# Two layers of one-token attention over a cache: uneven last rows of four loads, and W2's end laid over its start so that more keys stay

## The chip, the cores and the metric

The kernel runs on one core of one Trainium2 chip. Times are microseconds on the device. "Before" is the median of three runs, 1355.34 (1352.47 to 1356.29). A profile is one further execution, recorded by the hardware profiler.

## The reference

One token passes through two equal layers that share all weights and the cache. Each layer is attention with 32 heads over 8192 cached positions, then a small MLP:

```python
q = (layernorm(x) @ wq)                        # 640 -> 32 heads x 128
p = softmax(q . k_cache * 128 ** -0.5)         # per head, 8192 positions
x = x + (p @ v_cache) @ wo                     # 4096 -> 640
x = x + relu(layernorm(x) @ w1) @ w2           # 640 -> 1728 -> 640
```

All is float32. K and V of one head are 4 MiB each, so each layer reads 256 MiB of cache. Layer 1 walks the heads backwards, from 31 to 0, so that what layer 0 read last can stay in the chip's memory and serve layer 1 first.

## The kernel before

**The ring.** K, V and most of W2 are loaded into one big tile, `ring`, by SP's DMA queue (line 204). Its space is counted in *places* of 8 floats in each of 128 partitions, 4 KB. A head's data are cut into *units*, and a unit into *pieces*: a K piece `(r, c, n)` holds positions c to c+n of run r (four runs of 512 columns, for four groups of positions); a V piece holds a block of rows. Heads 2 to 26 are one unit of eight pieces of 256 places each, loaded in stretches of up to 64 KB per partition (`turning`); the other heads have several units. The table `UNITS` (lines 42 to 61) writes them out by hand, and the same table sets the layout in HBM, so that each load reads whole rows of up to 64 KB.

**What sets the order.** `todo` lists the loads in order. `pump` (line 190) issues from its head as long as the ring has room: at a fixed place (`turning`) or where `place` (line 166) finds a gap. Each `scores` and `values` call that has used a piece calls `release`, which frees its places and pumps again. So a load on SP's queue waits for PE's last use of the places that it overwrites, and for landed loads that the tile framework makes it wait for; everything behind it on SP's queue waits too. WQ and WO for groups of four heads come by ACT's queue.

**Kept heads.** `KEPT = 3800` places (lines 62, 63) hold heads 31 and most of 30 from layer 0 to layer 1. The rest of head 30's K, two units of 216 and 80 places' worth of columns, is loaded a second time at the boundary of the layers, into the tiles `mix` and `wct`, which are then free (`load_beside`, lines 806 and 845). `RING = KEPT + 960`: the last 960 places hold the twelve blocks of W2 that pass through the ring (80 places each, four runs of 4, 4, 2 and 2 blocks).

**The boundary.** When head 31's V has been used, the MLP follows: `hidden` with the last head's output (L603), WO of the last head and W2 by `times_rows` (L419), the ReLU (L824 to L850). W2's blocks are used in the order 0 to 3, two that have a tile of their own, 4 to 11 (line 859). Each use frees 80 places, into which layer 1's first loads (head 29) go. Then come the layer norm and the queries of layer 1, and the scores of head 31 from kept keys (L448).

**Compute.** Per head PE multiplies q with K (L448), DVE and ACT do the softmax (L459 to L489), PE multiplies with V (L497), DVE gathers (L512, L516). Other PE work is put between the heads.

Of the kernel before, what the change touches and what calls it, by code (L numbers as in the profile page):

```python
# [16 lines left out]
D = 640  # L17
H = 32
SK = 8192
DH = 128  # L20
DFF = 1728
# [24 lines left out]
UNITS[29] = [  # L46
    ("k", K_ALL[:1]),
    ("k", K_ALL[1:2]),
    ("k", [(2, 0, 512), (3, 0, 384)]),
    ("v", V_ALL[:1]),  # L50
    ("v", V_ALL[1:2]),
    ("k", [(3, 384, 128)]),
    ("v", V_ALL[2:3]),
    ("v", V_ALL[3:]),
]
UNITS[30] = [
    ("k", [(0, 432, 80), (1, 0, 80)]),
# [1 line left out]
    ("k", [(1, 80, 432)] + K_ALL[2:]),  # L59
] + HALVES[2:]  # L60
UNITS[31] = HALVES[:2] + LAST
DROPPED = {30: 2}
KEPT = 3800
MIX_AT = [12, 16, 20, 24]
AHEAD = 3

# [5 lines left out]
def kind_of(unit, t):  # L72

    return unit[0] if unit[0] != "kv" else "k" if t < len(K_ALL) else "v"


def wide(kind, piece):

    if kind == "w":
        return D // 8  # L80
    return 4 * piece[2] * (1 if kind == "k" else DH) // 8


def size(unit):
    return sum(wide(kind_of(unit, t), piece) for t, piece in enumerate(unit[1]))
# [4 lines left out]
F_TILES = 3  # L90
# [2 lines left out]
W2_RUNS = [range(0, 4), range(4, 8), range(8, 10), range(10, 12)]  # L93
UNITS["w2"] = [("w", list(run)) for run in W2_RUNS]
W2_ALL = [("w2", i) for i in range(len(W2_RUNS))]
RING = KEPT + 4 * F_TILES * D // 8


@with_exitstack
def decode_kernel(ctx: ExitStack, tc: tile.TileContext, x, kv, wq, wo, w1, w2, w2_rest, out):  # L100
    nc = tc.nc
# [11 lines left out]

    ring = consts.tile([P, 8 * RING], F32, name="ring")
    order = [(h, i) for h in range(H) for i in range(len(UNITS[h]))]
    kept = [u for u in order if u[0] >= min(DROPPED) and u[1] >= DROPPED.get(u[0], 0)]
    assert sum(size(UNITS[h][i]) for h, i in kept) == KEPT
    beside = [(1, u) for u in order if u[0] == 30 and u not in kept]
    todo = []

    def all_of(layer, u):
# [34 lines left out]
    source = {}  # L156
    for us, dram in ((order, kv), (W2_ALL, w2)):
        o = 0
        for u in us:
            n = 8 * P * size(UNITS[u[0]][u[1]])  # L160
# [5 lines left out]
    def place(layer, u, n):  # L166

        step = 512 if n % 512 == 0 else 8
        if layer:
            low, high = 0, RING  # L170
        elif u[0] in range(FULL[0]):
            low, high = 0, 16 * SLOT
        elif u[0] == "w2":
            low, high = KEPT, RING
        else:
            low, high = (3072, KEPT) if n == KEPT - 3072 else (0, 3072)
        at, best = low, None
        for a, m in sorted(live.values()) + [(high, 0)]:
            a = min(a, high)
            for base in (0, KEPT):  # L180
                c = base + -(-max(at - base, 0) // step) * step
                if a - c >= n and (best is None or a - at < best[1]):
                    best = c, a - at
            at = max(at, a + m)
        return None if best is None else best[0]

    def is_free(at, n):
        return all(a >= at + n or a + m <= at for a, m in live.values())

    def pump():  # L190
        while todo:
            layer, u, first, last, at = todo[0]
            unit = UNITS[u[0]][u[1]]
            ns = [wide(kind_of(unit, t), piece) for t, piece in enumerate(unit[1])]
            n = sum(ns[first:last])
            if at is None:
                at = place(layer, u, n)
                if at is None:
                    return
            elif not is_free(at, n):  # L200
                return
            todo.pop(0)
            o = 8 * sum(ns[:first])
            nc.sync.dma_start(ring[:, 8 * at : 8 * (at + n)], source[u][:, o : o + 8 * n])
            for t in range(first, last):
                live[layer, u, t] = at, ns[t]
                at_of[layer, u, t] = ring, 8 * at
                at += ns[t]

    def load_beside(where, at, n):  # L210
        layer, u = beside.pop()
        kind, pieces = UNITS[u[0]][u[1]]
        assert 8 * size(UNITS[u[0]][u[1]]) == n
        nc.sync.dma_start(where[:, at : at + n], source[u])
        for t, piece in enumerate(pieces):
            at_of[layer, u, t] = where, at
            at += 8 * wide(kind, piece)

    def key(L, u, t):
        return (0 if u in kept else L), u, t  # L220

    def release(L, u, t):
        if (L or u not in kept) and at_of[key(L, u, t)][0] is ring:
            del live[key(L, u, t)]
            pump()
# [13 lines left out]
    def load_wq(g, queue):  # L239
        wq_t[g] = wts.tile([P, NB, HG * DH], F32, name="wq_t")  # L240
        queue.dma_start(wq_t[g], wq[g])
# [3 lines left out]
        queue.dma_start(wo_t[g], wo[g])  # L245

    xr = work.tile([P, DR], F32, name="xr", bufs=2)
    nc.sync.dma_start(xr, x)
    load_wq(0, nc.sync)
    pump()  # L250
    load_wo(0, nc.sync)

# [23 lines left out]
    mix = consts.tile([P, DFF], F32, name="mix")  # L276
# [54 lines left out]
    def deviations(xt, s):  # L331
        pt = ps_m.tile([P, 512], F32, name="pm")
        nc.tensor.matmul(pt[:, :1], all_rows, s, start=True, stop=True)
        m = work.tile([P, 1], F32, name="ln_m")
        nc.vector.tensor_scalar(m, pt[:, :1], 1.0 / D, 0.0, op0=ALU.mult, op1=ALU.add)
        xc = work.tile([P, 2 * DH], F32, name="q_row")[:, :DR]
        nc.vector.tensor_scalar(xc, xt, m, 0.0, op0=ALU.subtract, op1=ALU.add)
        ss = work.tile([P, 1], F32, name="ln_ss")
        nc.vector.scalar_tensor_tensor(
            xc, xc, 1.0, xc, op0=ALU.mult, op1=ALU.mult, accum_out=ss  # L340
        )
        return ss

    def spread_of_rows(ss):
        pv = ps_m.tile([P, 512], F32, name="pm")
        nc.tensor.matmul(pv[:, :1], all_rows, ss, start=True, stop=True)
        return inv_std(pv[:, :1])
# [68 lines left out]
    def times_rows(acc, wt, col, first, last):  # L416

        for g in range(4):
            nc.tensor.matmul(  # L419
                acc[32 * g : 32 * g + 32, :DR],  # L420
                col.to_broadcast([col.shape[0], 32]),
                wt[:, g * DR : (g + 1) * DR],
                start=first,
                stop=last,
                skip_group_check=True,
            )
# [103 lines left out]
    def copied_rows(hd):  # L530

        rows = work.tile([P, 4, DH], F32, name="p")
        nc.vector.tensor_copy(rows[:, :2], hd.out[:, :2])
        nc.scalar.copy(rows[:, 2:], hd.out[:, 2:])
        return rows
# [64 lines left out]
    def hidden(ph, col, wt, first, last):  # L600
        for g in range(4):
            f, n = F_AT[g], F_ROWS[g]
            nc.tensor.matmul(  # L603
                ph[32 * g : 32 * g + 32, :n],
                col.to_broadcast([P, 32]),
                wt[:, f : f + n],
                start=first,
                stop=last,
                skip_group_check=True,
            )  # L610

    def attention_and_mlp(L, xr, s):
        heads = list(range(H))[:: 1 - 2 * L]
        last = heads[-1]
        runs = [heads[a : a + HG] for a in range(0, H, HG)]
        groups = [run[0] // HG for run in runs]
# [106 lines left out]
        for where, h in enumerate(heads[:-1]):  # L723
# [36 lines left out]
            k, j = divmod(where, HG)  # L760
# [36 lines left out]
        rows = copied_rows(hd)  # L797
        keep_busy(1, 128)
        o = work.tile([P, 1], F32, name="c_ol")
# [2 lines left out]

        xp, ph = mlp_in
        hidden(ph, o, mix, False, True)
        if L == 0:
            load_beside(mix, 0, DFF)
        pd = ps_m.tile([P, 512], F32, name="pm")
        times_rows(pd, wo_t[last // HG][:, last % HG], o, True, True)
        keep_busy(1, 128)
# [50 lines left out]
        for a, b in enumerate(blocks):  # L860
            if a == 2:
                ss = deviations(x1, s1)
            if a == 8:
                r1 = spread_of_rows(ss)
            rows = 2 * half if b == nb + 1 else P
            if b < nb:
                i = next(i for i, run in enumerate(W2_RUNS) if b in run)
                where = L, ("w2", i), b - W2_RUNS[i][0]
                tile_of, at = at_of[where]
                wt = tile_of[:, at : at + D]  # L870
            else:
                wt = w2_t[:rows, b - nb]
            times_rows(po, wt, hT[:rows, b : b + 1], a == 0, a == len(blocks) - 1)
            if b < nb:
                release(*where)

        x2 = work.tile([P, DR], F32, name="xr", bufs=2)
        s2 = work.tile([P, 1], F32, name="x_s", bufs=2)
# [7 lines left out]
    for L in range(2):  # L886
        xr, s = attention_and_mlp(L, xr, s)
# [80 lines left out]
```

## Time and profile before

| | |
|---|---|
| median of three runs | 1355.34 us |
| the profiled execution's own time | 1351.49 us |
| its span, first to last instruction | 1349.7 us |
| granted clock of TensorE | 0.81 |
| PE, DVE, ACT busy | 59%, 19%, 4% of the span |
| SP's DMA queue (q1) | 20312 packets, 531.89 MB |
| ACT's DMA queue (q10) | 4608 packets, 42.44 MB |

How to read it. The profile has a share of time in which the core's 16 DMA engines moved packets, for the span in 40 slices or for any stretch: 1.00 means that all 16 are busy, 0.50 that half of them are, or all of them half the time. The chain of waits is followed back from the last instruction to what released it. "us to landing" is the time from a DMA's issue to its last byte; most of it is standing in the queue behind older loads. The queues named "instruction" carry the program's own code.

### The profile page before, as it was taken

The numbers are of one execution on the slowest core, as the hardware profiler recorded it, in microseconds if no ns is written. First come the engines' busy times: TensorE is split into PE (matmuls) and PEld (weight loads), VectorE is DVE, ScalarE is ACT, GpSimd is POOL, SyncE is SP. The second block draws the span as 40 slices with busy tenths as digits, with TensorE's granted clock in tenths as the row PEclk, the third lists the DMA queues.
The fourth block names the chain that finished last, engine by engine and source line by source line (L and its number), as shares of the span: only waits on it lengthen the run. The fifth ranks groups of instructions, "written<-read, shape, count | busy, mean of one in ns | idle before, by whom it ended". The sixth has DMA issues, their size and how long they took to land.

```text
span 1349.7 us, 13544 instructions
## 1 busy us (share of the span) xinstructions
PE 799.3 (59%) x6048; PEld 270.4 (20%) x6048; DVE 251.4 (19%) x794; ACT 59.2 (4%) x149; POOL 2.9 (0%) x10
## 2 busy tenths in 40 slices
PE   5455555554654655457787754555566554656658
PEld 2011111211211211122242211111121121212214
DVE  1111111221211211122122211122111211111212
ACT  0000000000000000000000000000000000000000
POOL 0000000000000000000000000000000000000000
PEclk8777677878978976788799777797778778777879
DMA  9999999999999999999999999999999999999997
GB/s 392 445 419 437 432 428 441 417 431 436 439 426 432 430 435 422 448 417 420 425 405 423 435 431 432 432 431 436 438 434 424 421 435 443 429 420 438 429 418 322
DMA packets 24977, 575.17 MB, mean 426 GB/s; under 512 B 2772, under 2 KB 2904, under 8 KB 5336
## 3 DMA queue, kind: packets, MB, share of 16 engines
q1 hardware_dynamic: 20312, 531.89, 91.8%
q10 hardware_dynamic: 4608, 42.44, 7.5%
q8 instruction: 47, 0.77, 0.2%
q14 instruction: 10, 0.08, 0.0%
HBM read 574.31 MB, written 0.00 MB: 426 GB/s over the span
## 4 chain that ended last, share of the span: by engine, by line
DMA 65%; PE 27%; DVE 5%; issue 1%; ACT 1%; ACTq 0%; SPq 0%; DVEq 0%
DMA ring<-in_kv 64%; PE ps L448 13%; PE outs L497 8%; DVE h_t L459 2%; PE px L387 1%; DVE pt L477 1%; PE pm L464 1%; ACT p L473 1%; DMA wo_t<-in_wo 1%; DVE p L516 1%; PE acc L419 1%; PE px L419 1%; PE acc L603 0%; PE px L590 0%; DVE pT L479 0%
## 5 line engine op out<-in xcount | busy, mean ns | idle before, releaser
L448 PE MATMUL ps<-ring,spread_q 128*32 128x512 f32 (+2 forms) x2072 | 331.0, 787 | 334.5 <-DMA ring<-in_kv 329.6
L497 PE MATMUL outs<-ring,pT 128*4 128x512 f32 (+1 forms) x2080 | 268.2, 658 | 27.7 <-DVE pT L479 17.4
L448 PEld LDWEIGHTS ps<-ring,spread_q 128*32 128x32 f32 x2072 | 76.9, 138 | 523.2 <-issue 298.4
L459 DVE TENSOR_REDUCE h_t<-ps 128x1 f32<-128x512 f32 x64 | 44.3, 692 | 640.3 <-PE ps L448 640.3
L473 ACT ACTIVATE p<-ps,h_t 128x512 f32<-128x512 f32 x64 | 44.0, 687 | 1226.4 <-DVE h_t L471 1226.4
L497 PEld LDWEIGHTS outs<-ring,pT 128*4 128x4 f32 x2080 | 52.5, 92 | 184.4 <-issue 156.9
L526 PE MATMUL pm<-ones,p 128*128 128x1 f32 x120 | 22.9, 260 | 94.8 <-DVE p L516 94.8
L512 DVE TENSOR_SCALAR p<-outs,ind 128x128 f32<-128x128 f32 x60 | 21.1, 351 | 248.2 <-PE outs L497 248.2
L516 DVE SCALAR_TENSOR_TENSOR p<-outs,ind,p 128x128 f32<-128x128 f32 x180 | 63.1, 351 | 6.4
L477 DVE STREAM_TRANSPOSE pt<-p 128x512 f32<-128x512 f32 x64 | 46.5, 727 | 57.9 <-ACT p L473 57.9
L464 PE MATMUL pm<-row_of,h_t 128*128 128x16 f32 x128 | 25.7, 276 | 49.9 <-DVE h_t L459 49.0
L526 PEld LDWEIGHTS pm<-ones,p 128*128 128x128 f32 x120 | 17.8, 188 | 151.5 <-DVE p L516 149.9
L464 PEld LDWEIGHTS pm<-row_of,h_t 128*128 128x128 f32 x128 | 19.4, 190 | 109.2 <-DVE h_t L459 107.3
L590 PE MATMUL px<-w_t,wct 128*128 128x448 f32 (+1 forms) x80 | 36.6, 573 | 1.1 <-ACT wct L583 1.1
L387 PE MATMUL px<-wq_t,ln_xc 128*32 128x256 f32 x280 | 32.9, 381 | 0.0
L486 PE MATMUL pm<-ind,h_t 128*128 128x1 f32 x128 | 23.4, 252 | 15.3 <-ACT p L473 15.3
L486 PEld LDWEIGHTS pm<-ind,h_t 128*128 128x128 f32 x128 | 23.2, 207 | 34.1 <-ACT p L473 26.6
L419 PE MATMUL acc<-wo_t,o_cols 128*32 128x160 f32 x496 | 22.7, 324 | 0.6 <-DVE o_cols L544 0.6
L527 DVE TENSOR_SCALAR o_cols<-pm,h_t 128x1 f32<-128x1 f32 x60 | 13.1, 218 | 30.6 <-PE pm L526 30.6
L387 PEld LDWEIGHTS px<-wq_t,ln_xc 128*32 128x32 f32 x280 | 15.2, 109 | 12.7 <-issue 1.2
L471 DVE TENSOR_REDUCE h_t<-pm 128x1 f32<-128x16 f32 x64 | 11.2, 175 | 32.4 <-PE pm L464 32.4
L419 PEld LDWEIGHTS acc<-wo_t,o_cols 128*32 128x32 f32 x496 | 15.8, 117 | 4.8 <-issue 2.5
(110 smaller groups left out, 201.2 us busy)
## 6 DMA issues: line engine op xcount, KB each, us to landing
ring<-in_kv SPq DMA_DIRECT2D x20, 4096.0 KB, 34.5
ring<-in_kv SPq DMA_DIRECT2D x38, 2048.0 KB, 29.3
ring<-in_kv SPq DMA_DIRECT2D x11, 6144.0 KB, 38.2
wq_t<-in_wq ACTq DMA_DIRECT2D x14, 1280.0 KB, 23.4
wo_t<-in_wo ACTq DMA_DIRECT2D x14, 1280.0 KB, 23.8
ring<-in_kv SPq DMA_DIRECT2D x15, 1024.0 KB, 16.7
ring<-in_w SPq DMA_DIRECT2D x4, 1280.0 KB, 26.8
w_t<-in_w ACTq DMA_DIRECT2D x1, 4320.0 KB, 47.7
```

The source lines that it names most:

```text
L387: nc.tensor.matmul(pq[32 * j : 32 * j + 32, :n], xc[:, c : c + 1].to_broadcast([P, 32]), wq_t[g][:, c, j * n : (j + 1) * n], start=(c == 0 ...
L419: nc.tensor.matmul(acc[32 * g : 32 * g + 32, :DR], col.to_broadcast([col.shape[0], 32]), wt[:, g * DR : (g + 1) * DR], start=first, stop=last,
L448: nc.tensor.matmul(hd.ps[32 * g : 32 * g + 32, c : c + n], spread_q[:, 3 - r : 35 - r], tile_of[:, at + g * n : at + (g + 1) * n], start=f ...
L459: nc.vector.tensor_reduce(hd.nm, hd.ps, AX.X, ALU.max, negate=True)
L464: nc.tensor.matmul(pt[:, :16], hd.nm.to_broadcast([P, P]), row_of.rearrange("p g r -> p (g r)"), start=True, stop=True,)
L473: nc.scalar.activation(hd.p, hd.ps, AF.Exp, bias=hd.low, scale=1.0, accum_out=hd.l)
L477: nc.vector.transpose(pt, hd.p)
L486: nc.tensor.matmul(pt[:, :1], hd.l.to_broadcast([P, P]), ind[:, 4:5], start=True, stop=True)
L497: nc.tensor.matmul(hd.out[32 * g : 32 * g + 4, r : r + m].rearrange("p r d -> p (r d)"), hd.pT[:, 4 * i : 4 * i + 4], tile_of[:, v : v + m ...
L516: nc.vector.scalar_tensor_tensor(oc[:, r], hd.out[:, r], ind[:, r : r + 1], oc[:, r - 1], op0=ALU.mult, op1=ALU.add,)
L526: nc.tensor.matmul(pt[:, :1], oc[:, 3], ones, start=True, stop=True)
L590: nc.tensor.matmul(pt[:, :n], wct[:, c], w1_t[:, c, f : f + n], start=(c == 0), stop=(c == NB - 1),)
```

## The change

Five edits.

1. *More kept.* Head 29's K is cut anew, so that its last 320 columns of run 3 are a unit of their own, `(29, 9)`, of 160 places, loaded last. It is kept: `DROPPED` gains `29: 9`, `KEPT` goes from 3800 to 3960. Layer 1 doesn't load it again. The older K unit of 448 places becomes two of 128 and 160.
2. *W2 over itself.* `RING` is `KEPT + 800`: the same 4760 places in all. W2's last run (blocks 10 and 11) has no room until blocks 0 and 1 are used, in layer 0; then it goes over them.
3. *The second loads of head 30.* `beside` is turned round: wct's load comes first, at the place where it was; mix's, which was issued after `hidden`, comes after W2's second block.
4. *Uneven division.* Four loads (heads 9 and 15, in both layers) are split: all but the last 256 or 128 places of the stretch go in one DMA of 128 rows; those last places go in three DMAs of 64, 63 and 1 rows, or of 64, 51 and 13.
5. *x* is loaded by ACT's queue and not by SP's.

`place` and `apart` give the new units fixed homes. The core of the diff:

```diff
-    ("k", [(2, 0, 512), (3, 0, 384)]),
+    ("k", [(2, 0, 256)]),
+    ("k", [(2, 256, 256), (3, 128, 64)]),
...
-    ("k", [(3, 384, 128)]),
+    ("k", [(3, 0, 128)]),
...
+    ("k", [(3, 192, 320)]),
...
-DROPPED = {30: 2}
-KEPT = 3800
+DROPPED = {29: 9, 30: 2}
+KEPT = 3960
+W2_PLACES = 800
+SHARED = {
+    (0, 9): (SK // 32, [64, 63, 1]),
+    (0, 15): (SK // 64, [64, 51, 13]),
+    (1, 15): (SK // 32, [64, 63, 1]),
+    (1, 9): (SK // 64, [64, 51, 13]),
+}
...
-RING = KEPT + 4 * F_TILES * D // 8
+RING = KEPT + W2_PLACES
...
-            nc.sync.dma_start(ring[:, 8 * at : 8 * (at + n)], source[u][:, o : o + 8 * n])
+            tail, groups = SHARED.get((layer, u[0]), (0, [])) if last == len(unit[1]) else (0, [])
+            nc.sync.dma_start(
+                ring[:, 8 * at : 8 * (at + n - tail)], source[u][:, o : o + 8 * (n - tail)]
+            )
+            p = 0
+            for rows in groups:
+                nc.sync.dma_start(
+                    ring[p : p + rows, 8 * (at + n - tail) : 8 * (at + n)],
+                    source[u][p : p + rows, o + 8 * (n - tail) : o + 8 * n],
+                )
+                p += rows
...
-    nc.sync.dma_start(xr, x)
+    nc.scalar.dma_start(xr, x)
...
-        if L == 0:
-            load_beside(mix, 0, DFF)
...
+            if L == 0 and a == 1:
+                load_beside(mix, 0, DFF)
```

SP's queue at the boundary of the layers, before: the end of layer 0 with W2's four runs, the two second loads, and layer 1's first loads.

```order
L204 DMA ring<-in_kv 128x1024 x2
L204 DMA ring<-in_w 128x2560 x2
L204 DMA ring<-in_w 128x1280 x2
L214 DMA mix<-in_kv 128x1728
L214 DMA wct<-in_kv 128x640
L204 DMA ring<-in_kv 128x2048 x2
L204 DMA ring<-in_kv 128x3584
```

The same place in the changed kernel:

```order
L217 DMA ring<-in_kv 128x1024 x2
L217 DMA ring<-in_w 128x2560 x2
L217 DMA ring<-in_w 128x1280
L236 DMA wct<-in_kv 128x640
L217 DMA ring<-in_w 128x1280
L236 DMA mix<-in_kv 128x1728
L217 DMA ring<-in_kv 128x2048 x2
L217 DMA ring<-in_kv 128x1024
L217 DMA ring<-in_kv 128x1280
```

W2's last run stands behind wct's load, mix's behind both, and head 29's K unit of 3584 columns has become two.

SP's queue in layer 0 over the loads of heads 7 to 16, before:

```order
L204 DMA ring<-in_kv 128x16384 x4
L204 DMA ring<-in_kv 128x4096
L204 DMA ring<-in_kv 128x12288
L204 DMA ring<-in_kv 128x16384
L204 DMA ring<-in_kv 128x8192 x2
L204 DMA ring<-in_kv 128x16384
L204 DMA ring<-in_kv 128x12288
L204 DMA ring<-in_kv 128x4096
```

The same place in the changed kernel, from the third of the four long loads on:

```order
L217 DMA ring<-in_kv 128x14336
L222 DMA ring<-in_kv 64x2048
L222 DMA ring<-in_kv 63x2048
L222 DMA ring<-in_kv 1x2048
L217 DMA ring<-in_kv 128x16384
...
L217 DMA ring<-in_kv 128x3072
L222 DMA ring<-in_kv 64x1024
L222 DMA ring<-in_kv 51x1024
L222 DMA ring<-in_kv 13x1024
```

The third of the four long loads (head 9) and the last short one (head 15) are now four DMAs each, of which the last two have row counts that 16 doesn't divide.

More of the change, by code (lines that the diff above doesn't have):

```diff
@@ L117, in decode_kernel @@
     assert sum(size(UNITS[h][i]) for h, i in kept) == KEPT
-    beside = [(1, u) for u in order if u[0] == 30 and u not in kept]
+    apart = {(29, 9): (3800, KEPT), (30, 0): (4464, 4544), (30, 1): (4544, RING), (30, 2): (3072, 3800)}
+    beside = [(1, u) for u in order[::-1] if u[0] == 30 and u not in kept]
     todo = []
@@ L174, in place @@
             low, high = KEPT, RING
+        elif u in apart:
+            low, high = apart[u]
         else:
-            low, high = (3072, KEPT) if n == KEPT - 3072 else (0, 3072)
+            low, high = 0, 3072
         at, best = low, None
@@ L179, in place @@
             a = min(a, high)
-            for base in (0, KEPT):
+            for base in (0, 3328, KEPT):
                 c = base + -(-max(at - base, 0) // step) * step
```

## Prediction

> **What bounds the kernel now.** I read the page first: span, slices, queues, chain.
>
> ```profile
> span 1349.7 us, 13544 instructions
> ...
> PE 799.3 (59%) x6048; PEld 270.4 (20%) x6048; DVE 251.4 (19%) x794; ACT 59.2 (4%) x149; POOL 2.9 (0%) x10
> ...
> DMA  9999999999999999999999999999999999999997
> ...
> DMA packets 24977, 575.17 MB, mean 426 GB/s; under 512 B 2772, under 2 KB 2904, under 8 KB 5336
> ...
> q8 instruction: 47, 0.77, 0.2%
> ...
> HBM read 574.31 MB, written 0.00 MB: 426 GB/s over the span
> ...
> DMA 65%; PE 27%; DVE 5%; issue 1%; ACT 1%; ACTq 0%; SPq 0%; DVEq 0%
> ```
>
> The DMA engines are busy in every slice but the last: 575.17 MB at 426 GB/s, which is 26.6 GB/s (26.6 KB per us) for each of 16 engines. PE (59%) stands on the chain mostly because it frees places of the ring, which SP's queue waits for:
>
> ```profile
> SPq L204 <- PE outs L497: 555.4, 72, 15.2
> SPq L204 <- DMA ring<-in_kv: 552.3, 74, 22.2
> ```
>
> So the run lasts as long as the fullest DMA engine needs, plus a start and a tail. Whether "fullest" differs from "mean" is told by the table by stretches at the end:
>
> ```profile
> 1336.00:1339.00 3.00, 2.55 (x30) 1.60 (x26) 0.64 (x2) 0.37 (x1) 0.00 (x0) 1.00 1.01 418
> 1339.00:1340.00 1.00, 1.00 (x18) 0.53 (x10) 0.41 (x1) 0.00 (x0) 0.00 (x0) 1.00 0.71 292
> 1340.00:1341.00 1.00, 0.90 (x8) 0.76 (x8) 0.40 (x4) 0.37 (x2) 0.00 (x0) 1.00 0.57 241
> 1341.00:1342.00 1.00, 0.97 (x24) 0.70 (x24) 0.56 (x5) 0.00 (x0) 0.00 (x0) 1.00 0.48 200
> 1342.00:1343.00 1.00, 1.00 (x24) 0.94 (x26) 0.49 (x3) 0.00 (x0) 0.00 (x0) 1.00 0.53 206
> 1343.00:1344.00 1.00, 1.00 (x31) 0.49 (x26) 0.31 (x2) 0.00 (x0) 0.00 (x0) 1.00 0.39 164
> 1344.00:1345.00 1.00, 1.00 (x30) 0.72 (x22) 0.16 (x1) 0.00 (x0) 0.00 (x0) 1.00 0.11 46
> ```
>
> The last but one column is the DMA share. From 1340 to 1343 it stays near one half: about eight engines are done by 1340, the others work on until 1344 or so. Every load has 128 rows, so queue q1 gives all engines alike; what differs must be the 47 instruction packets. Their 0.2% of 16 x 1349.7 us is 43 us (32 to 54 with the rounding), 0.7 to 1.1 us each. On eight engines that is about six each, 4 to 7 us, which is the gap seen. From 1339 on the shares add to 2.8 us; shared evenly, all engines would end at 1341.8 and not at about 1344.6.
>
> At the very end a wait for data is still on the path, in the timeline:
>
> ```profile
> 1335.85 0.27 PEld L497 LDWEIGHTS outs<-ring,pT 128*4 128x4 f32 x8 [0.16 <-DMA ring<-in_kv]
> ...
> 1347.09 0.65 SPq L888 DMA_DIRECT2D out<-xr  x1
> ```
>
> The last block of V lands at 1335.8, and after it comes a fixed chain of 13.9 us to the end of the span. W2 lands inside that chain. So an engine that is late delays the end one for one.
>
> **The change part by part.** The profiled execution took 1351.49 us for its 1349.7 us of span; the median of the three runs is 3.85 us above it. I work out a difference on the profile and add it to the median. 0.3% is 4.07 us, about what a measurement of this kernel can tell from no change (its three runs lie 3.8 us apart).
>
> *Keys kept.* Head 29's last 320 positions stay from layer 0 to layer 1: one load of 128 x 1280 floats is gone, 640 KB. That is the size of a small W2 run:
>
> ```profile
> ring<-in_w SPq DMA_DIRECT2D x4, 640.0 KB, 20.8
> ```
>
> 655,360 bytes at 426 GB/s are **-1.54 us**, off every engine alike. No engine is idle over the layers, so the gain is whole, unless the boundary of the layers (below) eats it.
>
> *x on ACT's queue.* SP's first three issues:
>
> ```profile
> 0.74 0.39 SPq L248 DMA_DIRECT2D xr<-in_x  x1
> 1.19 0.41 SPq L241 DMA_DIRECT2D wq_t<-in_wq  x1
> 1.64 10.30 SPq L204 DMA_DIRECT2D ring<-in_kv  x8
> ```
>
> WQ and all behind it move up by 0.45 us. Bounds: -0.45 and 0, if x comes later from ACT and the first queries hold the ring back. I take **-0.4**, since ACT has nothing ahead of x.
>
> *Boundary of the layers.* W2's last run now waits until its first two blocks are used, wct's load goes ahead of it, mix's behind it. Rows of before:
>
> ```profile
> 694.00:696.00 2.00, 1.69 (x22) 0.90 (x21) 0.34 (x2) 0.00 (x0) 0.00 (x0) 1.00 1.02 422
> 696.00:697.00 1.00, 1.00 (x12) 0.94 (x8) 0.46 (x3) 0.37 (x2) 0.00 (x0) 1.00 0.90 336
> 697.00:698.00 1.00, 0.88 (x24) 0.80 (x25) 0.53 (x5) 0.00 (x0) 0.00 (x0) 1.00 0.83 289
> ...
> 701.00:702.00 1.00, 1.00 (x33) 0.96 (x36) 0.16 (x1) 0.00 (x0) 0.56 (x1) 1.00 0.93 286
> ```
>
> ```profile
> 667.66 15.01 SPq L204 DMA_DIRECT2D ring<-in_w  x4
> ...
> 697.60 0.72 PE L419 MATMUL px<-ring,hT 128*32 128x160 f32 x14
> ...
> 697.82 0.33 SPq L214 DMA_DIRECT2D wct<-in_kv  x1
> ...
> 700.96 1.84 PE L419 MATMUL px<-ring,hT 128*32 128x160 f32 x48
> ```
>
> ```profile
> ring<-in_kv SPq DMA_DIRECT2D x2, 1024.0 KB, 7.8
> ring<-in_kv SPq DMA_DIRECT2D x1, 1792.0 KB, 13.2
> ...
> DMA to landing us min/median/max: 19.1/25.8/47.7
> ...
> 702.86 0.33 SPq L204 DMA_DIRECT2D ring<-in_kv  x1
> ...
> 709.16 2.85 SPq L204 DMA_DIRECT2D ring<-in_kv  x4
> ```
>
> (The 19.1 us are the shortest landing among W1's and W2's loads.) Even now the DMA share falls to 0.83 there: the light engines run dry at about 696.1, the late ones do not. W2's last load is issued at 682.3 and lands 19.1 us later or more, at 701.5; without that last run (1.54 us) the late engines have work until about 699.9 and the light ones until 694.6. PE ends W2's first two blocks at 698.3 (697.60 + 0.72). SP can issue wct at 697.8 and the run at 698.3. On the late engines wct (320 KB) takes 0.77 us and the run 1.54: it lands near 702.2, or up to 0.6 later, an estimate: one more issue (0.33) and as much again for the start. PE wants it for the last two of the six blocks that begin at 700.96, at 702.2. So PE waits 0 to 0.6 us, and the late engines stand still for as long. The light engines lose about 4 us, but they were ahead by as much.
>
> The upper bound is the 7.8 us of the nearest loads issued in this stretch: the run lands at 706.1, PE is 3.9 us late. The first places of layer 1 are freed at 709.2 now, while the last load of the boundary lands at 716.1 (702.86 + 13.2). So 2 to 3 us at most reach the late engines. I take **+0.5**, between 0 and +2.5, near the low end because those 7.8 us hold the queue of older loads, which is shorter then. Layer 1's first loads stand behind this wait on SP's queue and find the same cover.
>
> *Uneven division.* Four times the last 64 rows of a piece go as 64, 63 and 1 rows of 8 KB, or 64, 51 and 13 rows of 4 KB. How engines share 63 or 51 rows no row shows; the only load or store here that isn't 128 rows is the last one:
>
> ```profile
> out<-xr SPq DMA_DIRECT2D x1, 2.5 KB
> ```
>
> One bound: as even as can be. Then an engine gains or loses one or two rows, at most 12 KB per layer, 0.46 us. The other: equal whole parts only, so 63 rows are 9 engines x 7, 51 rows 3 x 17, 13 rows 13 x 1. Then, against 96 KB when even, the first three engines carry 80 KB more in each layer (+3.1 us), the next six 12 KB more (+0.46), the last seven 44 to 48 KB less (-1.7 to -1.85).
>
> [...]
>
> What counts is the fullest engine, one with instruction packets. If it is among the last seven, it gets lighter; among the next six, 0.9 us heavier over both layers; among the first three, 6.1 us. Of eight such engines at least one is not among the last seven, so the maximum cannot fall by the full -1.7. I take **0**, between +0.9 and -0.9, for the forecast, and the far ends as rivals.
>
> [...]
>
> *The rest.* 19 more rows of SP's queue at 0.33 to 0.45 us each: SP only waits (552.3 us of it for earlier loads), so they cost nothing while two or more big loads are queued; without that cover each is 0.4 us.
>
> Two further score pieces per layer are 16 matmuls in all, on a PE that is busy 59%.
>
> Sum: -1.54 - 0.4 + 0.5 + 0 = -1.4 us; 1355.3 - 1.4 = **1353.9**.
>
> **The rivals.** *Overload (slower).* One of the first three engines also fetches instructions. It never idles, so 2 x 3.1 us come on top: -1.4 + 6.1 = +4.7, **1360.0**. For: if the eight are spread over the 16, or are the lower half, it must happen. Against: nothing in the trace numbers the engines, and if they are the upper half it can't; nor if rows are shared evenly. It decides once the added 80 KB meet about 2 us of packets in a layer.
>
> *Evened out (faster).* All engines with packets lie among the last seven, but one that has fewer. Then each layer's lead shrinks from about 4.5 us to the 3.1 us now on the first three: 1.7 to 2.8 us over the run, since the boundary takes part of it back. -1.4 - 2.2 = -3.6, **1351.7**. For: the last seven lose just about half of what the packets cost. Against: eight don't fit into seven.
>
> *Boundary eats it.* The run of W2 takes the 7.8 us, the queue runs dry in layer 1: +2.5 in place of +0.5, **1355.9**. For: light engines are already dry in 696 to 698. Against: the late ones aren't.
>
> **How the numbers follow.** Forecast 0.40, overload 0.33, evened out 0.20, boundary 0.07. Faster by over 4.07 us: a third of evened out and a tenth of the forecast's scatter, 0.12. Slower: overload lies 0.6 us over the bound, so six tenths of it, and a little of the boundary, 0.22. Within: 0.66. The range goes from -4.3 (evened out, full 2.8) to +5.2 (overload with the boundary's extra): 1351.0 to 1360.5. The forecast's own terms at their bounds give -2.9 to +1.9: 1352.4 to 1357.2.
>
> **What would show it.** HBM read 573.65 MB. At the end, shares by stretches: forecast, a half share of 4 to 5 us as now; evened out, a steep fall within 2 us; overload, a long low tail of 0.1 to 0.2 for 3 us more. At the boundary a share below 0.6 from 695 to 699, and a PE wait for the ring of under 1 us before the last blocks of W2. I am wrong if PE waits there by more than 3 us, if the last V lands later although no engine has a tail, or if layer 1 shows gaps in which all engines stand.

## The result, and the profile after

The changed kernel takes 1371.67 us (median of 4 runs, 1369.90 to 1373.72) beside 1354.20 us (4 runs) for the kernel before. The ratio is 1.0133, 95% interval 1.0119 to 1.0147: it is slower by about 18 us, outside the predicted range. The profiled execution took 1369.9 us.

The page of the changed kernel: span, share and rate of the DMA engines by slices, and the queue totals.

```profile
span 1368.1 us, 13640 instructions
...
DMA  9999999999999999999999999999999999999997
GB/s 396 433 434 428 436 434 367 427 431 434 388 426 437 435 424 424 440 422 422 426 373 423 428 439 427 428 441 427 433 417 369 428 439 417 414 414 441 433 418 323
DMA packets 26039, 574.54 MB, mean 420 GB/s; under 512 B 2937, under 2 KB 3069, under 8 KB 6397
...
q1 hardware_dynamic: 21228, 531.15, 91.7%
q10 hardware_dynamic: 4752, 42.52, 7.6%
...
HBM read 573.65 MB, written 0.00 MB: 419 GB/s over the span
```

The rate row and the two queues of the kernel before:

```profile
GB/s 392 445 419 437 432 428 441 417 431 436 439 426 432 430 435 422 448 417 420 425 405 423 435 431 432 432 431 436 438 434 424 421 435 443 429 420 438 429 418 322
...
q1 hardware_dynamic: 20312, 531.89, 91.8%
q10 hardware_dynamic: 4608, 42.44, 7.5%
```

The share row is as full as before, and the packets of the two queues fill 99.3% of the engines' span in both kernels. The packet records say it in time: summed over all packets and divided by 16 engines, they last 1344.7 us of 1349.7 before and 1361.6 of 1368.1 after. So of the 18.4 us by which the profiled span is longer, 16.9 are packets that take longer (for 0.6 MB less data) and 1.5 are engines that stand. The rate falls in single slices, the 7th, 11th and 31st above all (a slice is 34.2 us), and these lie at three of the four split loads. At the fourth (head 9 of layer 1) it is 363 GB/s from 1158 to 1162 us and 278 from 1162 to 1167, beside 459 and 419 before. The low 21st slice (373 beside 405) is the boundary of the layers: the same kernel without the division, e1_no_div below, has 361 there. So the place to look is not a wait. It is busy engines that move less. The table by stretches shows it at heads 9 and 15 of layer 0 and at head 15 of layer 1 (the last two columns are the DMA share and GB/s; a share a little above 1 means that packets overlap, up to 22 at a time on the 16 engines). Before:

```profile
224.00:230.00 6.00, 0.00 (x0) 0.00 (x0) 0.00 (x0) 0.00 (x0) 0.00 (x0) 0.73 1.05 449
230.00:236.00 6.00, 5.18 (x32) 1.32 (x32) 0.35 (x1) 0.00 (x0) 0.00 (x0) 0.70 1.08 465
...
360.00:366.00 6.00, 4.66 (x40) 1.56 (x38) 1.56 (x7) 0.00 (x0) 0.00 (x0) 1.00 1.00 429
...
1022.00:1029.00 7.00, 6.18 (x58) 2.13 (x54) 0.87 (x2) 0.45 (x1) 0.00 (x0) 0.75 1.03 442
1029.00:1036.00 7.00, 5.37 (x54) 1.86 (x43) 2.60 (x8) 0.33 (x2) 0.00 (x0) 1.00 1.02 437
```

After:

```profile
224.00:230.00 6.00, 0.66 (x6) 0.35 (x10) 0.22 (x1) 0.00 (x0) 0.00 (x0) 0.55 0.95 265
230.00:236.00 6.00, 5.79 (x32) 1.36 (x24) 0.15 (x1) 0.00 (x0) 0.00 (x0) 0.60 1.07 267
...
360.00:366.00 6.00, 4.61 (x41) 2.12 (x31) 2.29 (x5) 0.78 (x2) 0.00 (x0) 1.00 1.13 311
...
1022.00:1029.00 7.00, 4.71 (x40) 1.73 (x40) 2.02 (x8) 0.00 (x0) 0.00 (x0) 1.00 0.93 231
1029.00:1036.00 7.00, 2.58 (x15) 0.60 (x18) 0.00 (x0) 0.00 (x0) 0.00 (x0) 0.58 0.97 215
```

The share stays near 1.00 while the rate is half to three quarters of what it was. From 1022 to 1036 the kernel before moves 7 x (442 + 437) = 6153 KB and the changed one 7 x (231 + 215) = 3122 KB. The missing 3031 KB are 7.1 us at 427 GB/s, in one place of four.

### The profile page after: what moved, and what is told of

Its sections match the earlier page's. It is cut to its first block, busy times and chain, and to the rows that moved or that the text cites. A ratio compares the mean times of both kernels' runs of the same rounds, so it can differ in the third digit from the quotient of the medians.

```text
span 1368.1 us, 13640 instructions
## 1 busy us (share of the span) xinstructions
PE 792.2 (58%) x6080; PEld 270.5 (20%) x6080; DVE 251.6 (18%) x794; ACT 59.1 (4%) x149; POOL 2.9 (0%) x10
## 3 DMA queue, kind: packets, MB, share of 16 engines
HBM read 573.65 MB, written 0.00 MB: 419 GB/s over the span
## 4 chain that ended last, share of the span: by engine, by line
DMA 65%; PE 27%; DVE 5%; issue 1%; ACT 1%; ACTq 0%; SPq 0%; DVEq 0%
DMA ring<-in_kv 65%; PE ps L470 13%; PE outs L519 7%; DVE h_t L481 2%; PE px L409 2%; DVE pt L499 1%; PE pm L486 1%; PE px L441 1%; ACT p L495 1%; DVE p L538 1%; PE acc L441 0%; PE acc L625 0%; PE px L424 0%; DVE pT L501 0%; PE pm L508 0%
## 5 line engine op out<-in xcount | busy, mean ns | idle before, releaser
L470 PE MATMUL ps<-ring,spread_q 128*32 128x512 f32 (+3 forms) x2104 | 329.9, 775 | 354.1 <-DMA ring<-in_kv 348.8
L519 PE MATMUL outs<-ring,pT 128*4 128x512 f32 (+1 forms) x2080 | 257.4, 635 | 30.5 <-DVE pT L501 18.3
L409 PE MATMUL px<-wq_t,ln_xc 128*32 128x256 f32 x280 | 35.7, 405 | 0.0
L612 PEld LDWEIGHTS px<-w_t,wct 128*128 128x128 f32 x80 | 13.8, 197 | 9.1 <-issue 7.5
```

The costliest lines, as they stand in the source:

```text
L409: nc.tensor.matmul(pq[32 * j : 32 * j + 32, :n], xc[:, c : c + 1].to_broadcast([P, 32]), wq_t[g][:, c, j * n : (j + 1) * n], start=(c == 0 ...
L470: nc.tensor.matmul(hd.ps[32 * g : 32 * g + 32, c : c + n], spread_q[:, 3 - r : 35 - r], tile_of[:, at + g * n : at + (g + 1) * n], start=f ...
L519: nc.tensor.matmul(hd.out[32 * g : 32 * g + 4, r : r + m].rearrange("p r d -> p (r d)"), hd.pT[:, 4 * i : 4 * i + 4], tile_of[:, v : v + m ...
L612: nc.tensor.matmul(pt[:, :n], wct[:, c], w1_t[:, c, f : f + n], start=(c == 0), stop=(c == NB - 1),)
```

## The experiments

Unless the text says otherwise, each kernel is the kernel before with one edit, and each ratio is against runs of the kernel before on the same chip. In microseconds, 0.1% is 1.35.

**Which part of the change.** In e1_no_div the changed kernel loses its uneven division and keeps all else:

```diff
-SHARED = {(0, 9): (SK // 32, [64, 63, 1]), ...}
+SHARED = {}
```

> The changed kernel without its uneven division (the four loads whole again, everything else as changed). Theory HALF (a DMA that reaches only half of the partitions slows all engines) and theory LUMP (few engines carry 63 or 51 rows): both say that the division costs the whole loss, so 1352 to 1356 us, within 0.3% of before. Rival BOUNDARY (the late last run of W2 costs the time): 1365 us or more.

Measured: 1353.42 us, ratio 0.9996 (0.9985 to 1.0007). The rest of the change is worth -0.5 us (-2.0 to +0.9). Against this kernel the division costs 1.0133 / 0.9996, 1.37% or 18.5 us; with both intervals, 16 to 21.

In e2_div_only the kernel before gets nothing but the division, with the changed kernel's table and its three DMAs per part.

> The kernel before with the uneven division alone (64, 63, 1 and 64, 51, 13 rows at the same four loads). HALF and LUMP: +16 to +18 us, 1370 to 1373. BOUNDARY: within 0.3% of before.

Measured: ratio 1.0159 (1.0132 to 1.0185), +21.5 us, at 1377.24 a little above the 1370 to 1373 expected. So the division alone carries the loss. Its page also tells how the rows are shared:

```profile
q1 hardware_dynamic: 20940, 531.89, 91.4%
```

Before there were 20312 packets. If each DMA has a packet per row and one more per engine, the bulk of a stretch that is left counts as before, and the parts add 2 x (128 + 16 + 9 + 1) for 64, 63 and 1 rows and 2 x (128 + 16 + 3 + 13) for 64, 51 and 13: 628, which is 20940 (e3_cut_whole and e4_halves below come out the same way, at 20888 and 20952). The page's packets under 512 B, 2888 beside 2772, are 116 more, which is one per engine by the same count: 2 x (16 + 9 + 1) and 2 x (16 + 3 + 13). With the rows as even as can be it would be 20980. So the counts fit 63 rows on 9 engines and 51 rows on 3, as in the prediction's second bound: equal whole parts only.

**Which property of the division.** e3_cut_whole cuts off the same last places and loads them in one DMA of 128 rows; e4_halves in two of 64:

```diff
-    (0, 9): (SK // 32, [64, 63, 1]),
+    (0, 9): (SK // 32, [128]),        # e3_cut_whole
+    (0, 9): (SK // 32, [64, 64]),     # e4_halves
```

> The kernel before, the same four tails cut off but loaded in one DMA of 128 rows each. HALF and LUMP: nothing, 1352 to 1356 us. Rival CUT (more DMAs, and rows in HBM that no longer lie end to end, slow the engines): +5 us or more.

> The kernel before, the four tails in two DMAs of 64 rows, so that each DMA can use all 16 engines evenly but reaches half of the partitions. HALF: half rate for 2 x 1 MB and 2 x 0.5 MB, 7 us by that alone and up to the whole +17: 1361 to 1371. LUMP: nothing, 1352 to 1356.

Measured: e3_cut_whole 1.0010 (0.9999 to 1.0022), e4_halves 1.0128 (1.0108 to 1.0148), +17.3 us (14.6 to 20.0). The cut costs a tenth of a percent, two tenths at most by the interval. Halves, which by the packet count give all 16 engines the same number of rows, cost nearly all. Uneven engines are thus not needed for the loss. The stretches of e4_halves at head 9, layer 0:

```profile
224.00:230.00 6.00, 0.61 (x4) 0.23 (x8) 0.22 (x1) 0.00 (x0) 0.00 (x0) 0.78 0.87 233
230.00:236.00 6.00, 5.39 (x32) 1.26 (x24) 0.54 (x1) 0.00 (x0) 0.00 (x0) 0.65 1.12 286
236.00:242.00 6.00, 4.22 (x20) 1.35 (x24) 1.43 (x6) 0.78 (x2) 0.00 (x0) 0.63 0.95 406
```

The part is 1 MB, 2.5 us of transfer at full rate, and yet for 12 us the rate is 55% and 67% of 427. The slowness takes in other loads that are under way. The packet records show both: at this place the 128 rows of 8 KB take 518 ns each on average, beside 313 in e3_cut_whole; of the whole rows beside them, the seven of 56 KB that start between 224 and 228 us take 3.0 us beside 2.1, and the nine of 64 KB that start between 232 and 236 us 3.7 beside 2.4.

**Neighbouring or alternate partitions.** e5_alternate keeps two DMAs of 64 rows with the same bytes, but takes every second row; e6_quarters takes four DMAs of 32 neighbouring ones:

```diff
-                    ring[p : p + rows, ...], source[u][p : p + rows, ...],
+                    ring[p::2, ...], source[u][p::2, ...],     # e5_alternate, p = 0, 1
```

> The kernel before with the four last parts cut off as in e4_halves, in two DMAs of 64 rows each, but of every second row: the same number of DMAs, rows, bytes and rows per engine (4 rows by 16 engines, twice), and each DMA now reaches partitions from 0 to 127. PARTITIONS (the loss of e4_halves, 18 us, comes from writing to one half of the partitions only): no loss, 1354 to 1356. SIZE (it comes from DMAs of 64 rows as such, their number, or rows of another length beside the big ones): as e4_halves, about 1372.

> As e4_halves, but in four DMAs of 32 neighbouring partitions (0 to 31, 32 to 63, 64 to 95, 96 to 127), which go to 16 engines with 2 rows each. [...] PARTITIONS (slowed by the share of the partitions that it reaches, a quarter here): about twice the loss or more, 1385 to 1395. SIZE: more than halves, since there are eight more DMAs.

Measured: e5_alternate 1.0005 (0.9992 to 1.0018), no loss; e6_quarters 1.0109 (1.0081 to 1.0136), as halves: 1369 us, where PARTITIONS had 1385 to 1395 and SIZE more than halves. So it isn't the size or the number of DMAs, nor does a quarter of the partitions cost more than a half. The same stretches of e5_alternate:

```profile
224.00:230.00 6.00, 1.81 (x10) 0.58 (x14) 0.22 (x1) 0.00 (x0) 0.00 (x0) 0.79 0.85 353
230.00:236.00 6.00, 5.19 (x30) 1.38 (x22) 0.69 (x1) 0.00 (x0) 0.00 (x0) 0.64 1.19 511
236.00:242.00 6.00, 4.23 (x28) 1.12 (x31) 1.27 (x5) 0.78 (x2) 0.00 (x0) 0.72 1.01 437
```

(353 and 511 have a mean of 432; the kernel before has 449 and 465 in these two stretches and 426 over its span.) The rows of 8 KB take 312 ns here, as in e3_cut_whole.

**Does the loss go with the bytes?** e7_half_dose halves the parts of e4_halves (`SK // 64`, `SK // 128`).

> As e4_halves, but with half of the bytes in the parts that are cut off (4 KB and 2 KB of each row instead of 8 and 4). RATE (these bytes move at a lower rate): half of the loss, 1363. EVENT (each such DMA throws the engines out of step once, and the full DMAs behind it pay for that): as e4_halves, about 1372. In between, both have a part.

Measured: 1.0066 (1.0039 to 1.0092), +8.9 us (5 to 12), half of e4's 17.3. It goes with the bytes (RATE); the 17 of EVENT lies outside the interval.

**Uneven, but nearly all partitions.** e8_lump_all_rows has `[117, 3, 3, 3, 2]` in place of `[64, 64]`.

> As e4_halves, but each part that is cut off goes in DMAs of 117, 3, 3, 3 and 2 rows: by the rule that the number of engines divides the rows, 13 engines take 9 rows and then the first two or three take the 11 others, so per layer the first three engines carry 48 to 60 KB more than an even share, the last three 96 KB less. Nearly all bytes are in a DMA that reaches 117 of 128 partitions. HALF: the loss is nearly gone, only the first engines' overload is left: 1354 to 1360 (the 60 KB more per layer at the 26.6 GB/s of one engine are 2.3 us per layer). LUMP (uneven engines cost the whole difference): 1372 or more.

Measured: 1.0114 (1.0086 to 1.0143), +15.4 us (11.6 to 19.3). HALF had 1354 to 1360 here and got 1370: writing 117 of the 128 partitions in one DMA didn't help. The 20920 packets fit 13, 3, 3, 3 and 2 engines for the five DMAs; which engines these are the trace doesn't tell. Nor is it mainly the uneven engines: of the 18.3 us by which the profiled span is longer than before, 15.7 are packets that take longer and 2.6 are engines that stand. A longer stretch shows the rates.

**A sustained stretch.** e9 to e11 and e13 to e16 load all four heads 9 to 12 of layer 0 in the way under test, whole rows, 33.6 MB:

```diff
-            nc.sync.dma_start(ring[:, 8 * at : 8 * (at + n)], source[u][:, o : o + 8 * n])
+            for rows in SHARED.get((layer, u[0]), [P]):
+                nc.sync.dma_start(ring[p : p + rows, ...], source[u][p : p + rows, ...])
+                p += rows
```

with `[64, 64]` in e9_heads_halves, `[117, 11]` in e10_heads_117, `[120, 8]` in e11_heads_120 and `[96, 32]` in e16_heads_96_32. Counted as in e2_div_only, the packets of these four (20392, 20352, 20347 and 20392, beside 20312 before; five loads are divided) fit 16 engines for 64, 96 and 32 rows, 13 for 117, 11 for 11, 15 for 120 and 8 for 8. 13 and 11 are more than 16 together, so some engine of e10 carries 9 + 1 rows of a load where 8 are an even share, and some engine of e11 8 + 1: the 10/8 and 9/8 of LUMP, if it is the same one each time. e9 and e16 are even.

> The kernel before, with the loads of heads 9, 10, 11 and 12 of layer 0 (8.39 MB each, 19.7 us each at 427 GB/s) in two DMAs, rows 0 to 63 and rows 64 to 127, whole rows and not only their ends. A sustained stretch, so that the rate can be read without the neighbours. OVERLAP (the second half starts on the engines that are ahead, so both halves are written at once): little loss, below 20 us. HALF (they go one after the other, each at half the rate): +79 us, 1433. THIRD (the parts cut off in e4_halves cost 17 to 18 us where half the rate would have cost 7.4, which is 30% of the rate): +180 us, 1535.

> [...] LUMP alone: 10/8 of the time, +19.7 us for four heads, 1374. [...]

> [...] LUMP alone: 9/8 of the time, +9.8 us for four heads, 1364. [...]

> As e9_heads_halves, but in DMAs of 96 and 32 neighbouring rows: 16 engines with 6 rows each, then 16 with 2, so every engine carries an even share. [...]

Measured (two runs each): halves 1.0719 (1.0700 to 1.0739), +97 us; 117 and 11 rows 1.0729 (1.0661 to 1.0797), +99; 120 and 8 rows 1.0972 (1.0952 to 1.0992), +132; 96 and 32 rows 1.0764 (1.0691 to 1.0837), +103. The table by stretches, 260 to 280 us, of the kernel before:

```profile
260.00:280.00 20.00, 11.12 (x92) 4.15 (x89) 6.82 (x17) 1.25 (x4) 0.00 (x0) 0.95 0.99 427
```

of e9_heads_halves:

```profile
260.00:280.00 20.00, 9.51 (x58) 2.42 (x50) 3.58 (x11) 0.78 (x2) 0.00 (x0) 0.76 1.01 198
```

of e10_heads_117:

```profile
260.00:280.00 20.00, 4.38 (x36) 1.35 (x36) 2.71 (x9) 0.51 (x2) 0.00 (x0) 0.75 0.81 268
```

of e11_heads_120:

```profile
260.00:280.00 20.00, 10.13 (x70) 3.01 (x70) 3.58 (x11) 0.78 (x2) 0.00 (x0) 0.79 0.90 186
```

and of e16_heads_96_32:

```profile
260.00:280.00 20.00, 8.27 (x54) 2.05 (x46) 3.58 (x11) 0.78 (x2) 0.00 (x0) 0.76 1.01 222
```

In e9_heads_halves busy engines (1.01) move 198 GB/s: 46% of 427. HALF's price of 79 us holds to within a quarter; OVERLAP (below 20) and THIRD (+180) are out. Neither fewer nor more neighbours do better: quarters cost about what halves do (1.0109 beside 1.0128), and in e16, where the first DMA writes 96 partitions and every engine has an even share, the rate is about as low (222 GB/s). The divisions into 117 and 11 and into 120 and 8 rows are uneven. LUMP alone had 1374 and 1364 for them; 1452 and 1485 were measured, 120 rows the worst of all. Engines do stand in these two: by the packet records 31.9 us of the span in e10 and 20.1 in e11, beside 5.0 in the kernel before, 5.7 in e9 and 8.2 in e16. That is some 27 and 15 us for LUMP, which had 19.7 and 9.8; the rest of the loss is longer packets. Why they are longer no run here takes apart. What is shown: of the divisions tried here, full rate comes only with 128 rows in one DMA and with alternate rows.

**The write or the read.** e13 takes alternate rows of source and partitions; e14 takes alternate source rows into halves of the partitions; e15 takes halves of the source into alternate partitions. In e14 and e15 the rows of these heads land in other partitions, so the output isn't the reference's; only the transfers are of use.

```diff
+SHARED = {(0, h): list(zip(HALF, ALTERNATE)) for h in range(9, 13)}     # e14: to, of
...
+                nc.sync.dma_start(ring[to, ...], source[u][of, ...])
```

> As e9_heads_halves (+97 us), but the two DMAs of 64 rows take every second row, of the source and of the partitions alike, over whole rows of heads 9 to 12. If what e5_alternate showed for short rows holds for a sustained stretch: no loss, 1352 to 1358. If it was the shortness of the stretch that hid a loss there: +20 us or more.

> As e9_heads_halves, but the rows 0, 2, 4 and so on of the source go to partitions 0 to 63, and the odd ones to 64 to 127, so that only the destination is a half (the rows of heads 9 to 12 then stand in other partitions, and the output is not the reference's). DESTINATION (the writes into one half of the partitions are what is slow): +97 us, 1450. SOURCE (reading 64 neighbouring rows, 4 MB in one piece, is what is slow): no loss, 1354.

> The other way round: rows 0 to 63 of the source go to the even partitions, rows 64 to 127 to the odd ones (again other rows in other partitions). DESTINATION: no loss, 1354. SOURCE: +97 us, 1450.

Measured: e13 1.0007 (0.9992 to 1.0023), e14 1.0703 (1.0658 to 1.0747), e15 0.9993 (0.9979 to 1.0006). Stretch 260 to 280 us of e14_to_halves:

```profile
260.00:280.00 20.00, 10.49 (x58) 2.56 (x50) 3.59 (x11) 0.78 (x2) 0.00 (x0) 0.67 1.03 206
```

and of e15_from_halves:

```profile
260.00:280.00 20.00, 12.05 (x88) 3.81 (x84) 5.40 (x16) 1.01 (x4) 0.00 (x0) 0.91 1.02 440
```

This settles it for 64 rows: the partitions that are written decide, 206 GB/s against 440, and the rows that are read don't matter (1.0703 of the time with halves written, 0.9993 with halves read).

**Many small DMAs.** e12_eight_light sends the last 4 KB of each row of two loads in 16 DMAs of 8 rows each, every fourth partition of 32:

```diff
+                q = 32 * (p // 32) + p % 32 // 8
+                nc.sync.dma_start(ring[q : q + 29 : 4, ...], source[u][q : q + 29 : 4, ...])
```

> [...]

Measured: 1.0164 (1.0150 to 1.0177), +22 us. The 20824 packets fit 8 engines for each of the small DMAs. The time doesn't tell what such a division is worth by itself, since another wait came in: of the 26.8 us by which its profiled span is longer, 3.1 are packets that take longer and 23.7 are engines that stand. A stretch at head 9, then SP's queue in the timeline:

```profile
232.00:236.00 4.00, 2.92 (x22) 0.73 (x14) 0.86 (x2) 0.00 (x0) 0.00 (x0) 0.92 0.09 30
```

```profile
208.95 30.35 SPq L215 DMA_DIRECT2D ring<-in_kv  x13
```

Here the engines nearly all stand (share 0.09): SP spends 30 us in the line that issues the small DMAs, and the loads behind them come late. The longest of that line's waits, over both places:

```profile
SPq L215 <- DMA ring<-in_kv: 27.9, 3, 16.1
```

Another 32.6 us of it are put down to loads of WQ and WO. So SP waits there for earlier loads to land before it issues a small DMA; why the program has it wait for these loads, no run here takes apart.

No version here beat both kernels; e1_no_div equals the kernel before within its interval.

## Why the prediction was wrong, point by point

- **Uneven division: the step that failed.** "I take **0**, between +0.9 and -0.9"; the far ends were -2.2 and +6.1. It cost 18.5 us (16 to 21). Both bounds counted rows per engine (the second with a slip: an engine that comes first in every part, as it supposes, also takes the single row of 8 KB, so 88 KB more in each layer and not 80) and gave each row the duration that it has in a DMA of 128 rows. The second bound's count of engines fits (20940 packets); which engines take the rows no run shows. The duration wasn't: how fast a row is written depends on which partitions its DMA writes (206 GB/s in e14, 440 in e15), and the whole rows under way beside it are slowed too (3.7 us beside 2.4 in e4_halves); 16.9 of the 18.4 us are packets that take longer. The row that should have warned me was already quoted: "the only load or store here that isn't 128 rows is the last one". I bounded the unknown sharing and took the unknown rate as known, with no bound on it at all.
- **Size of it.** At half the rate the 3.1 MB of e4_halves would cost 7.4 us more; 17.3 were measured. The packet records show where the rest is. I summed the times of all packets of 2 KB and more and divided by 16 engines: e4_halves has 16.0 us more than e3_cut_whole, which has the same rows, 5.1 in packets of 2, 4 and 8 KB and 10.9 in the others, nearly all of it in longer rows, the whole rows beside them. So rows of ordinary DMAs are slowed as well while such parts are under way.
- **Overload (the slower rival).** The sign was its sign, not its mechanism: halves with even engines lose as much as 117 rows with uneven ones (+97 us in e9, +99 in e10). What the uneven engines add, 21.5 less 17.3 us, is within the intervals of e2 and e4. The profiled execution of e2 also took some 5 us more than before from its last V block to its end, where its granted clock was mostly 0.50 and before had 1.00, so even that difference need not be transfer.
- **Keys kept.** HBM read is 573.65 MB, as said. As for x, WQ's issue now stands at 0.73 us where it stood at 1.19. SP's queue has 14 more issues, 156 beside 142, and not 19. None of these can be told apart in the time.
- **Boundary.** In e1_no_div, where no other loss overlies it, the stretches show the predicted dip, but a share below 0.6 in one stretch only (the third column from the end is TensorE's granted clock):

```profile
694.00:696.00 2.00, 1.69 (x22) 0.99 (x21) 0.25 (x2) 0.00 (x0) 0.00 (x0) 1.00 0.75 312
696.00:698.00 2.00, 1.88 (x27) 1.66 (x24) 0.88 (x4) 0.37 (x2) 0.00 (x0) 0.84 0.52 210
698.00:700.00 2.00, 2.00 (x26) 1.42 (x22) 0.77 (x6) 0.00 (x0) 0.00 (x0) 0.50 0.62 182
```

The timeline of e1_no_div shows W2's last run issued at 699.17, 0.9 us later than I said, and PE at the blocks that need it with no wait noted. That is no confirmation of a wait of under 1 us: PE came to these blocks 2.8 us later than before (703.73 and not 700.96), since its clock had fallen to 0.50 and W2's blocks took nearly twice as long (these 48 matmuls 3.43 us and not 1.84). The prediction has no term for the clock. The fall isn't the change's own: e2_div_only, with the old boundary, has 0.50 and 3.43 us there too, e5_alternate 1.00. How much of the dip it adds isn't shown.

```profile
699.17 0.33 SPq L212 DMA_DIRECT2D ring<-in_w  x1
...
703.73 3.43 PE L436 MATMUL px<-ring,hT 128*32 128x160 f32 x48
```

- **Sum of all but the division.** -1.4 us predicted, -0.5 (-2.0 to +0.9) measured: it holds, but so would 0.
- **The end.** The forecast wanted a half share of 4 to 5 us at the end; the changed kernel falls from 0.63 to 0.16 within a microsecond:

```profile
1359.00:1360.00 1.00, 0.88 (x23) 0.80 (x26) 0.47 (x5) 0.00 (x0) 0.00 (x0) 1.00 0.71 292
1360.00:1361.00 1.00, 1.00 (x25) 0.67 (x21) 0.49 (x6) 0.00 (x0) 0.00 (x0) 1.00 0.63 242
1361.00:1362.00 1.00, 1.00 (x32) 0.53 (x20) 0.62 (x3) 0.00 (x0) 0.00 (x0) 1.00 0.16 67
```

So the engines do end closer together, as *Evened out* had it. Two other ends tell what brought it, as far as one profile of each can. e4_halves, slow as well but with even rows, keeps a half share:

```profile
1357.00:1358.00 1.00, 1.00 (x19) 0.50 (x7) 0.42 (x1) 0.06 (x1) 0.00 (x0) 1.00 0.71 297
1358.00:1359.00 1.00, 0.88 (x10) 0.82 (x10) 0.48 (x3) 0.30 (x2) 0.00 (x0) 1.00 0.54 225
1359.00:1360.00 1.00, 1.00 (x25) 0.68 (x25) 0.46 (x4) 0.00 (x0) 0.00 (x0) 1.00 0.54 225
1360.00:1361.00 1.00, 1.00 (x26) 0.88 (x26) 0.60 (x3) 0.00 (x0) 0.00 (x0) 1.00 0.46 180
1361.00:1362.00 1.00, 1.00 (x28) 0.56 (x24) 0.19 (x2) 0.00 (x0) 0.00 (x0) 1.00 0.20 82
```

e2_div_only falls as the changed kernel does, from 0.64 (1360 to 1362 us) to 0.17, 0.13 and 0.04. So the steep end goes with the uneven rows and not with the slow stretches. Its gain, about 2 us by the prediction, is hidden below a loss eight times as large.

**What stays open.** Which rows each engine takes in these DMAs: the trace doesn't number the engines. And why 96, 117 and 120 neighbouring rows are as slow as 64 or slower (+103, +99 and +132 us beside +97), while 64 alternate ones lose nothing (1.0007): no run here takes that apart.

## What to carry to other kernels

When a load is divided by rows, ask what each division writes, not only how much each engine carries: give the duration of a row in a new shape bounds of its own, down to half the rate or less (198 GB/s of 427 in e9_heads_halves), and bounds for the rows beside it too (3.7 us beside 2.4 in e4_halves). A DMA share near 1.00 says that engines are occupied, not that they move bytes (1.01 at 198 GB/s in e9_heads_halves); read GB/s beside it, stretch by stretch. If rows must be divided, try alternate partitions first (1.0005 and 1.0007 of the time here), and measure the division alone before combining it with other edits.

## What the runs showed of the hardware

- Loads to 64 neighbouring partitions ran at 198 GB/s where loads to 128 run at about 427, with the engines busy (a share of 1.01 from 260 to 280 us); to every second partition, two such DMAs ran at full rate (1.0007 of the time).
- DMAs of 96 and 32, 117 and 11, and 120 and 8 neighbouring partitions cost as much as halves or more (+103, +99 and +132 us on four heads, beside +97). By its packet count (20392) the first gives all engines the same number of rows; in the other two some 27 and 15 us are engines that stand.
- Such parts slow whole rows under way beside them: beside the halves of e4_halves nine rows of 64 KB took 3.7 us each where they took 2.4 in e3_cut_whole.
- The loss lies on the side of the partitions that are written: halves of the source into alternate partitions cost nothing (0.9993), alternate rows of the source into halves of the partitions 1.0703 of the time.
- Sixteen DMAs of 8 rows in a row kept SP's queue for 30 us, mostly in waits for earlier loads to land (over two such places 27.9 us for loads of the ring and 32.6 for WQ and WO), and the engines fell to a share of 0.09 behind it.
